# Down projection in batches of six and five chunks, with one ring of small staged parts: attention and a gated FFN on one core

## The chip, the cores and the metric

The kernel runs on one core of a Trainium2 chip. The metric is the device time of one execution in microseconds. Before the change it is 1235.75 us, the median of three runs (1235.59 to 1236.77). The profile is of one execution, and every duration below is from that one.

## What is computed

The reference, cut to its core (B = 1, S = 2048, D = 512, 32 heads of 16, F = 1376, all fp32):

```python
q = (x @ wq).reshape(B, S, H, Dh).transpose(0, 2, 1, 3)
k, v = x @ wk, x @ wv                      # one head of keys and values for all 32
p = softmax(einsum("bhqd,bkd->bhqk", q, k) * Dh ** -0.5)
a = einsum("bhqk,bkd->bhqd", p, v).transpose(0, 2, 1, 3).reshape(B, S, H * Dh) @ wo
b = (gelu(x @ w_gate) * (x @ w_up)) @ w_down
g = sigmoid((x * gate_w).sum(-1, keepdims=True))
return g * a + (1 - g) * b
```

## The kernel before, in words

Each fp32 matrix is held as two halves in a shorter format, high (`...h`) and low (`...l`), and a product is three matmuls: high by high, high by low, low by high. A *split* makes the halves: DVE casts to the high half (L201), and GpSimd (POOL) subtracts it from the source for the low half (L202).

The 2048 rows are four groups of 512. The FFN's 1376 columns are 11 chunks of 128 a group, 44 in all; a chunk has a gate part, an up part (the two *g parts*) and a down part (the *d part*), 256 KB each. The first 80 us make keys, values, queries (which go out to DRAM, `scr`), the first chunk of each group and the first FFN product. Then comes the loop, on which the change works. It interleaves, on TensorE (PE), three streams:

- **S and Z**, scores: two matmuls (L750) fill two PSUM banks with scores of 128 keys by 1024 queries, and ACT takes their exp (L753). S uses the first two pairs of banks in turn, Z the third.
- **V**, values: eight matmuls (L820) add one 128-key step to the attention result. 32 *units* of 16 steps each (four heads by 512 queries) make all 512 steps. When a unit's last V has run, `norm` has DVE copy the result out of its one PSUM bank (L764 or L774) and queues some ten small operations for later.
- **F**, projection steps: a z and a y matmul on the upper and the lower half of PE's rows, side by side (L518).

F steps belong to *jobs*: a **gate job** (24 F) makes one chunk's gate and up products, followed by GELU on ACT and DVE (L543 to L559); a **down job** multiplies a batch of finished chunks by their down weights, for two of the four row tiles of the group, and DVE adds the result to `acc` (L621, L623); a **wo job** (24 F) is the output projection of attention. Batches are of 3, 3, 3 and 2 chunks a group; with two jobs a batch and 3 terms by 2 halves a chunk, a down job has 18 or 12 F.

The second half of a job swaps the two row halves, so that each must wait until both matmul streams of the first half are through. That wait goes over a **relay**: an empty instruction on the SyncE queue (SP) that waits for PE, and that PE waits for in turn (L520 to L529). SP takes its instructions in the order in which they were recorded. It also issues all transfers: weights (L314), pieces of x and wo (L335), the six transfers that load the next unit's queries, called the *Q load* (L363, L364, L369), and the output (L634). The Q load is recorded at the score that is the fifth of a unit's 32.

The order of it all is a list, `PLAN`, one line a job: `H` opens it, `F3` is three F steps, `S`, `Z`, `V2` are as above, `R` closes the job and hands its result to DVE, and `T` starts the GELU's tanh. Visits are unbroken runs of V. After every third F comes a *slot* (L530, L531), in which one queued piece of DVE work is recorded: a split from `todo`, else a piece of wo from `lazy`, else a piece of the norm from `bg`. In the first half of a gate job only the first two of the four slots may take a split.

Weights are staged a chunk at a time, 768 KB in one transfer into one of two buffers (`fetch_w`, L308). A gate job n records the fetch of chunk n + 2 ahead of its first F (L584), and queues the splits of chunk n + 1 two scores later (L587). x and wo come in pieces of 256 KB through two buffers of their own (`fetch_split`, L332).

Of the kernel before, what the change touches and what calls it, by code (L numbers as in the profile page):

```python
# [9 lines left out]
F32 = mybir.dt.float32  # L10
# [4 lines left out]
ALU = mybir.AluOpType  # L15
# [27 lines left out]
PB = 12  # L43
PLAN = [
# [82 lines left out]
def mix_kernel(ctx, tc, xT, wq, wo, wf, out):  # L127
# [51 lines left out]
    st0 = cp.tile([P, 3, D], F32, tag="st", name="st0", bufs=2)  # L179
# [120 lines left out]
    W = {}  # L300
    stage = {0: st0}
# [6 lines left out]
    def fetch_w(n):  # L308
        if n < len(chunks):
            stage[n] = cp.tile([P, 3, D], F32, tag="st", name=f"st{n}", bufs=2)  # L310
            r = chunks[n][1]
            w = wf[(r - 1) % NF].rearrange("p (t d) -> p t d", t=3)
            t0 = 0 if r else 2
            nc.sync.dma_start(stage[n][:, t0:3], w[:, t0:3])  # L314

    def split_w(n):
        if n not in stage:
            return []
        st = stage.pop(n)
        dh = cp.tile([P, D], F32R, tag="dh", name=f"dh{n}", bufs=4)  # L320
        dl = cp.tile([P, D], F32R, tag="dl", name=f"dl{n}", bufs=4)
        parts = [(dh, dl, st[:, 2])]
        gh = gl = None
        if chunks[n][1]:
            gh = cp.tile([P, 2, NC, P], F32R, tag="gh", name=f"gh{n}", bufs=2)
            gl = cp.tile([P, 2, NC, P], F32R, tag="gl", name=f"gl{n}", bufs=2)
            view = lambda t: st[:, t].rearrange("p (c f) -> p c f", c=NC)
            parts = [(gh[:, t], gl[:, t], view(t)) for t in range(2)] + parts
        W[n] = gh, gl, dh, dl
        return [lambda part=part: split(nc.vector, nc.gpsimd, *part) for part in parts]  # L330

    def fetch_split(name, src, dst, queue):  # L332
        def fetch(c):
            t = cp.tile([P, D], F32, tag="xst", name=f"{name}{c}", bufs=2)
            nc.sync.dma_start(t, src[:, c])  # L335
            return t

        parts = {c: fetch(c) for c in range(2)}

        def go(c):  # L340
            hi, lo = dst()
            split(nc.vector, nc.gpsimd, hi[:, c], lo[:, c], parts.pop(c))
            if c + 2 < NC:
                parts[c + 2] = fetch(c + 2)

        queue.extend(lambda c=c: go(c) for c in range(NC))

    def reload_x(tg):
        xs.pop(tg)

        def dst():
            if tg not in xs:
                xs[tg] = x_tiles(tg)
            return xs[tg]

        fetch_split(f"xst{tg}_", xT[tg], dst, todo)
# [19 lines left out]
    def h_tiles(n):  # L376
        return [cp.tile([P, TG], F32R, tag=t, name=f"{t}{n}", bufs=3) for t in ("hh", "hl")]
# [558 lines left out]
```

## Time and profile before

| | us |
|---|---|
| median of three runs (lowest, highest) | 1235.75 (1235.59, 1236.77) |
| the profiled execution's own time | 1235.6 |
| its span, first to last instruction | 1233.8 |
| busy: PE | 1226.5 |
| busy: ACT | 1028.3 |
| busy: DVE | 548.2 |
| busy: POOL | 213.4 |
| span ahead of the loop, loop, end | 80.2, 1137.5, 16.1 |

Busy time is the union of an engine's instructions; a share of 99% says that the engine had always something under way, not that it worked at its peak. A row of the timeline gives start, duration, engine, line, operation, names and shapes, and how many follow each other (xN); brackets hold the idle time ahead of it and what ended it. A row of the waits gives the total, the count and the longest. PEld is PE's weight load, and SPq is SP's own queue.

### The profile page before, as it was taken

To read this page: it belongs to the slowest core of one execution; us is meant where nothing else is said; L and a number is where in the kernel's file an instruction comes from. 1 tells how busy PE (TensorE), PEld (TensorE's weight loads), DVE (VectorE), ACT (ScalarE), POOL (GpSimd) and SP (SyncE) were. 2 spreads that over 40 slices of the span, in tenths; PEclk is the share of its full clock that TensorE was granted. 3 is DMA by queue.
4 is the path that set the end of the run, shared out by engine and by line. 5 is a ranking of instruction groups with operands and counts; after the bars stand their busy time and mean duration, and the time that the engine had idled before them with its cause. 6 is when DMAs were issued, how large, how long until landed. Compare 5 with 4: busy or idle time off the path is not lost.

```text
span 1233.8 us, 23557 instructions
## 1 busy us (share of the span) xinstructions
PE 1226.5 (99%) x9742; PEld 663.7 (54%) x9742; DVE 548.2 (44%) x844; ACT 1028.3 (83%) x1127; POOL 213.4 (17%) x188
## 2 busy tenths in 40 slices
PE   9999999999999999999999999999999999999998
PEld 7875455545454455544545555555555545555555
DVE  7862652533552063543346135343544333344334
ACT  5449899889898888898988888888888888888884
POOL 5411411211220021120222012021123002112100
PEclk9999999999999999999999999999999999999999
DMA  8541202102110110210220012110131011020000
GB/s 332 197 148 57 83 1 66 40 23 99 58 40 15 68 58 15 66 41 23 61 97 27 32 57 66 40 48 33 35 112 45 32 57 60 21 66 27 15 1 35
DMA packets 28317, 73.89 MB, mean 60 GB/s; under 512 B 4208, under 2 KB 4464, under 8 KB 28208
## 3 DMA queue, kind: packets, MB, share of 16 engines
q1 hardware_dynamic: 27664, 71.32, 17.4%
q8 instruction: 77, 1.26, 0.5%
q0 software_dynamic: 256, 0.79, 0.2%
q10 hardware_dynamic: 288, 0.26, 0.1%
q14 instruction: 32, 0.26, 0.1%
HBM read 57.41 MB, written 14.94 MB: 59 GB/s over the span
## 4 chain that ended last, share of the span: by engine, by line
PE 92%; DVE 1%; ACT 1%; issue 0%; ACTq 0%
PE acc L820 38%; PE s L750 23%; PE z L518 15%; PE y L518 15%; PE wos L504 1%; ACT p L753 1%; DVE acc L633 0%; DVE sq L547 0%; PE wof L504 0%; DVE nz L780 0%; DVE sq L546 0%; DVE nt L783 0%; ACT sq L550 0%; DVE gs L543 0%; DVE n L774 0%
## 5 line engine op out<-in xcount | busy, mean ns | idle before, releaser
L753 ACT ACTIVATE p<-s 128x1024 f32<-128x1024 f32 x1024 | 974.9, 1025 | 144.6 <-PE s L750 134.6
L820 PE MATMUL acc<-p,v 128*32 128x512 f32 x4096 | 490.2, 598 | 0.0
L750 PE MATMUL s<-Q,kp 51*128 51x512 f32 x2048 | 376.8, 418 | 1.5 <-DMA Q<-scr 1.2
L750 PEld LDWEIGHTS s<-Q,kp 51*128 51x128 f32 x2048 | 183.1, 184 | 237.4 <-ACT p L753 149.8
L202 POOL TENSOR_TENSOR gl<-st,gh 128x512 fp32r<-128x512 f32 x80 | 112.3, 1423 | 753.1 <-PE s L750 390.8
L820 PEld LDWEIGHTS acc<-p,v 128*32 128x32 f32 x4096 | 110.8, 109 | 244.5 <-issue 236.0
L518 PE MATMUL z<-xh,gh 64*128 64x512 f32 x312 | 123.0, 394 | 0.0
L518 PE MATMUL y<-xh,gh 64*128 64x512 f32 x312 | 123.0, 394 | 0.0
L518 PE MATMUL z<-xl,gh 64*128 64x512 f32 x312 | 122.1, 391 | 0.8 <-POOL xl L202 0.7
L518 PE MATMUL y<-xl,gh 64*128 64x512 f32 x312 | 122.3, 392 | 0.0
L518 PE MATMUL y<-xh,gl 64*128 64x512 f32 x312 | 121.9, 391 | 0.0
L518 PE MATMUL z<-xh,gl 64*128 64x512 f32 x312 | 121.9, 391 | 0.0
L543 DVE COPY gs<-z 128x512 f32<-128x512 f32 x39 | 27.0, 691 | 200.8 <-PE z L518 122.7
L202 POOL TENSOR_TENSOR dl<-st,dh 128x512 fp32r<-128x512 f32 x44 | 57.6, 1309 | 79.9 <-DVE dh L201 50.6
L518 PE MATMUL z<-dh,hh 64*128 64x512 f32 x176 | 69.2, 393 | 0.0
L518 PE MATMUL y<-dh,hh 64*128 64x512 f32 x176 | 69.1, 392 | 0.0
L518 PE MATMUL y<-dl,hh 64*128 64x512 f32 x176 | 68.8, 391 | 0.0
L518 PE MATMUL z<-dh,hl 64*128 64x512 f32 x176 | 68.7, 390 | 0.0
L518 PE MATMUL y<-dh,hl 64*128 64x512 f32 x176 | 68.7, 390 | 0.0
L518 PE MATMUL z<-dl,hh 64*128 64x512 f32 x176 | 68.6, 390 | 0.0
L623 DVE SCALAR_TENSOR_TENSOR acc<-z,gc,acc 128x512 f32<-128x512 f32 x24 | 18.0, 751 | 109.1 <-PE z L518 69.5
L518 PEld LDWEIGHTS z<-xl,gh 64*128 64x128 f32 x312 | 58.1, 186 | 7.4 <-POOL xl L202 1.7
(173 smaller groups left out, 1498.5 us busy)
## 6 DMA issues: line engine op xcount, KB each, us to landing
st<-wf SPq DMA_DIRECT2D x40, 768.0 KB
scr<-q SPq DMA_DIRECT2D x16, 512.0 KB
Q<-scr SPq DMA_DIRECT2D x64, 128.0 KB
Q<-scr SPq DMA_DIRECT2D x64, 64.0 KB
out<-acc SPq DMA_DIRECT2D x16, 256.0 KB
xr<-xT SPq DMA_DIRECT2D x6, 512.0 KB
xst<-xT SPq DMA_DIRECT2D x12, 256.0 KB
st<-wf SPq DMA_DIRECT2D x5, 256.0 KB
```

Source lines behind the costliest of these rows:

```text
L202: eng_l.tensor_sub(lo, src, hi)
L504: nc.tensor.matmul(ps, a, b, start=(first and q == 0), stop=(last and q == len(terms) - 1), skip_group_check=True)
L518: mm = nc.tensor.matmul(ps, a[rs], b[rs], start=(half == 0 and q == 0), stop=(half == 1 and q == len(X) - 1), skip_group_check=True)
L543: nc.vector.tensor_copy(gs, g)
L623: nc.vector.scalar_tensor_tensor(o, ps, w, o, op0=ALU.mult, op1=ALU.add)
L750: nc.tensor.matmul(ps[:, j * TG : (j + 1) * TG], kp[rs, kc * P : (kc + 1) * P], Q[u][rs, pr], start=True, stop=True)
L753: nc.scalar.activation(p, ps, AF.Exp, bias=0.0, scale=SCALE)
L820: nc.tensor.matmul(accp[u][32 * j : 32 * j + 32], vt[:, kc], pb[s, j // 2][:, (j % 2) * TG : (j % 2 + 1) * TG], start=(kc == 0), stop=(kc ...
```

## The change

- Down jobs come in two batches a group, of six chunks (36 F) and five (30 F): 16 down jobs instead of 32, and 61 jobs in all instead of 77. The buffers follow: six pairs of `dh`, `dl` and of `hh`, `hl`, four and three of them in one pool and the rest in another. `acc` has one buffer, not two, and the norm uses `n0` and `n1` in place of `nt`.
- Staging is one ring of four buffers of 256 KB. Its parts are the two g parts of chunk n + 1, the d part of chunk n itself, a piece of wo in four of the jobs, and four pieces of x at a group's end. Three parts are fetched ahead. Splitting a part records the next fetch at once, into the buffer of the part that was split before it.
- Every slot may take a split, and the splits of a job are queued as it opens.
- `PLAN` is written anew, with 1608 F, 1024 S and Z and 512 V as before.

The core of the diff:

```diff
-    "f: H F3 S F3 S F6 S2 F6 S F3 S F3 R S V Z S T S V4 S Z S V2 S",
+    "f: H F3 S F3 S F4 S F2 S F3 S F3 S F3 S F3 R S V S Z T S V4 Z S2 V2 S",
...
+    def parts(n):
+        r = n % NF
+        m = n + 1 if r < NF - 1 else n + 2
+        p = [("g", m, t) for t in range(2)] if m < len(chunks) else []
+        if n > 2:
+            p += [("d", k, 0) for k in ([n] if r > 1 else [n - 1, n])]
+        if 3 <= n < 3 + NC:
+            p.append(("o", 0, n - 3))
+        return p
...
+    def fetch():
+        while supply and len(raw) < STAGE - 1:
+            p = supply.pop(0)
+            t = cp.tile([P, D], F32, tag="st", name="st", bufs=STAGE)
+            nc.sync.dma_start(t, source(*p))
+            raw.append((p, t))
+
+    def split_part(p):
+        q, t = raw.pop(0)
+        assert p == q
+        split(nc.vector, nc.gpsimd, *target(*p), t)
+        done.add(p)
+        fetch()
...
     def slot(split_too):
-        for q in (todo, lazy, bg) if split_too else (bg,):
+        for q in (todo, bg) if split_too else (bg,):
...
                 if q % EVERY == EVERY - 1 and (half == 0 or q + 4 <= len(X)):
-                    slot(half == 1 or q + 6 <= len(X))
+                    slot(True)
...
         def begin():
             flush(todo)
-            if n == 2:
-                fetch_w(3)
-            fetch_w(n + 2)
-            if n == 3:
-                fetch_split("wo", wo, lambda: (woh, wol), lazy)
-            defer(5 if n == 2 else 2, lambda: todo.extend(split_w(n + 1)))
-            if r == NF - 1:
-                defer(3, lambda: todo.extend(split_w(n + 2)))
+            queue_parts(parts(n))
             return weights_terms(n, 0), weights_terms(n, 1)
...
-                acc[tg] = mp.tile([P, 4, D], F32, tag="acc", name=f"acc{tg}", bufs=2)
+                acc[tg] = mp.tile([P, 4, D], F32, tag="acc", name=f"acc{tg}", bufs=1)
...
-            if r % 3 == 2 or r == NF - 1:
+            if r == 5 or r == NF - 1:
```

What this moves shows on SP and on DVE around a gate job that follows the end of a unit. On SP before, in the middle of the loop; `st31` and `st32` are the weights of two chunks, `Q22` the queries of a unit, and the brackets hold what a transfer waits for. The relay itself isn't listed, but its wait for PE is: it stands as PE_49 on the first fetch behind it.

```order
L314 DMA st31_9189<-wf 128x1536 [waits PE_49,DMAHW0_49,Pool_49]
L363 DMA Q22_9200<-scr_71 32x2x512 [waits DMAHW1_49,PE_49]
L364 DMA Q22_9200<-scr_71 16x2x512 [waits DMAHW2_49]
L363 DMA Q22_9200<-scr_71 32x2x512 [waits DMAHW3_49]
L364 DMA Q22_9200<-scr_71 16x2x512 [waits DMAHW4_49]
L369 DMA Q22_9200<-shs_72 3x2x512 [waits DMAHW5_49]
L369 DMA Q22_9200<-shs_72 3x2x512 [waits DMAHW6_49]
L314 DMA st32_9349<-wf 128x1536 [waits PE_49,DMAHW7_49,Pool_49]
```

Between the relay of one job (PE_49 at `st31`) and that of the next (PE_49 at `st32`) stand one fetch, right behind the first relay, and the Q load. On SP after, around a job of the same kind; the `st` rows are single parts.

```order
L349 DMA st_3109<-wf 128x512 [waits PE_49,DMAHW7_49,DMAHW3_49,Pool_49]
L349 DMA st_3124<-wf 128x512 [waits DMAHW4_49,DMAHW0_49,Pool_49]
L367 DMA Q6_3126<-scr_71 32x2x512 [waits DMAHW5_49,PE_49]
L368 DMA Q6_3126<-scr_71 16x2x512 [waits DMAHW6_49]
L367 DMA Q6_3126<-scr_71 32x2x512
L368 DMA Q6_3126<-scr_71 16x2x512
L373 DMA Q6_3126<-shs_72 3x2x512 [waits DMAHW1_49]
L373 DMA Q6_3126<-shs_72 3x2x512 [waits DMAHW2_49]
L349 DMA st_3148<-wf 128x512 [waits DMAHW3_49,Pool_49]
L349 DMA st_3296<-xT 128x512 [waits PE_49,DMAHW4_49,Pool_49]
```

Between the two relays (PE_49 at `st_3109` and at `st_3296`) there are three fetches now, each with a wait for POOL, and the Q load stands between the second and the third. On DVE before, at the job of `st31`: `n020` is the copy of the finished unit's result, `gh30` and `dh30` are high halves of the next chunk.

```order
L764 COPY n020_9180<-acc20_8891 128x512
L765 TENSOR_SCALAR nt20_9181<-n020_9180,mk_80 128x512
L766 TENSOR_SCALAR nz20_9182<-n020_9180,mkb_81 128x512
L201 CAST gh30_9221<-st30_9005 128x512 x2
L201 CAST dh30_9219<-st30_9005 128x512
```

On DVE after, at the job of `st_3124`, with the high halves of chunk 10 and of chunk 9's d part:

```order
L758 COPY n04_3089<-acc4_2815 128x512
L186 CAST gh10_3105<-st_2898 128x512
L186 CAST gh10_3105<-st_2913 128x512
L186 CAST dh9_3144<-st_2930 128x512
L759 TENSOR_SCALAR nz4_3090<-n04_3089,mkb_81 128x512
L760 TENSOR_SCALAR n04_3089<-n04_3089,mk_80 128x512
```

The casts come right behind the copy, ahead of the norm's two products. The copy is still ahead of the casts, and so ahead of POOL's subtractions, on which the fetches above wait.

More of the change, by code (lines that the diff above doesn't have):

```diff
@@ L43 @@
 PB = 12
+STAGE = 4
 PLAN = [
     "t: S2",
[77 rows of a table removed]
[61 rows of a table added]
 ]
@@ L178, in mix_kernel @@
     xr = {tg: p2.tile([P, NC, TG], F32, tag="xr", name=f"xr{tg}", bufs=4) for tg in order[:3]}
-    st0 = cp.tile([P, 3, D], F32, tag="st", name="st0", bufs=2)
+    st0 = p2.tile([P, 3, D], F32, tag="st0", name="st0", bufs=1)
     wf0 = wf[LASTF].rearrange("p (t d) -> p t d", t=3)
@@ L299, in mix_kernel @@
     chunks = [(tg, r) for tg in range(NTG) for r in range(NF)]
-    W = {}
-    stage = {0: st0}
+    G = {}
+    DW = {}
+    todo = []
     now = [-1]
@@ L306, in defer @@
         later.setdefault(now[0] + k, []).append(fn)
[L308 to L356, printed above, removed]
+    def g_tiles(n):
+        G[n] = [cp.tile([P, 2, NC, P], F32R, tag=t, name=f"{t}{n}", bufs=2) for t in ("gh", "gl")]
+    def d_tiles(n):
+        pool, bufs = (cp, 4) if n % 6 < 4 else (mp, 2)
+        DW[n] = [pool.tile([P, D], F32R, tag=t, name=f"{t}{n}", bufs=bufs) for t in ("dh", "dl")]
@@ new lines, in target, with source @@
+    def target(kind, n, c):
+        if kind == "g":
+            if n not in G:
+                g_tiles(n)
+            return [w[:, c].rearrange("p c f -> p (c f)") for w in G[n]]
+        if kind == "d":
+            d_tiles(n)
+            return DW[n]
+        if kind == "x":
+            if c == 0:
+                xs[n] = x_tiles(n)
+            return [x[:, c] for x in xs[n]]
+        return woh[:, c], wol[:, c]
+    def source(kind, n, c):
+        if kind == "x":
+            return xT[n, :, c]
+        if kind == "o":
+            return wo[:, c]
+        t = 2 if kind == "d" else c
+        return wf[(chunks[n][1] - 1) % NF][:, t * D : (t + 1) * D]
@@ new lines, in parts, with x_parts @@
+    def parts(n):
[7 more added lines that the diff above has]
+        return p
+    def x_parts(tg):
+        return [("x", tg, c) for c in range(NC)]
+    supply = [("d", 0, 0), ("g", 1, 0), ("g", 1, 1), ("d", 1, 0), ("g", 2, 0), ("g", 2, 1), ("d", 2, 0)]
@@ new lines, in mix_kernel @@
+    for n, (tg, r) in enumerate(chunks):
+        if r and n > 1:
+            supply += parts(n)
+            if r == NF - 1 and tg + 1 < NTG:
+                supply += x_parts(tg + 1)
+    raw = []
+    done = set()
+    def fetch():
[10 more added lines that the diff above has]
+        fetch()
@@ L358, in mix_kernel, with queue_parts @@
+    def queue_parts(ps):
+        todo.extend(lambda p=p: split_part(p) for p in ps)
     Q = {}
@@ L376, in h_tiles @@
     def h_tiles(n):
-        return [cp.tile([P, TG], F32R, tag=t, name=f"{t}{n}", bufs=3) for t in ("hh", "hl")]
+        pool = mp if n % 2 else cp
+        return [pool.tile([P, TG], F32R, tag=t, name=f"{t}{n}", bufs=3) for t in ("hh", "hl")]
     first = {}
@@ L411, in halves @@
         def halves():
-            hh, hl = h_tiles(NF * tg)
+            hh, hl = h_tiles(0)
             for h in (hh, hl):
@@ L428, in mix_kernel @@
     hold = []
-    fetch_w(1)
+    supply.pop(0)
+    d_tiles(0)
+    fetch()
     for ti, tg in enumerate(order):
@@ L453, in mix_kernel @@
             if ti == 0 and b == 3:
-                split_w(0)[0]()
+                split(nc.vector, nc.gpsimd, *DW[0], st0[:, 2])
+                done.add(("d", 0, 0))
             if ti == 1 and b < 3:
-                if b == 0:
-                    parts = split_w(1)
-                parts[b]()
-                if b == 2:
-                    fetch_w(2)
-            if ti == 2 and b < 2:
-                if b == 0:
-                    parts = split_w(2)
-                parts[b]()
-                if b == 1:
-                    rest = parts[2]
+                split_part((("g", 1, 0), ("g", 1, 1), ("d", 1, 0))[b])
+            if ti == 2 and b < 2:
+                split_part(("g", 2, b))
             if last and b == 2:
@@ L486, in mix_kernel @@
     O = {}
-    todo = []
     bg = []
     chain = []
-    lazy = []
     def slot(split_too):
-        for q in (todo, lazy, bg) if split_too else (bg,):
+        for q in (todo, bg) if split_too else (bg,):
             if q:
@@ L530, in pair_mm @@
                 if q % EVERY == EVERY - 1 and (half == 0 or q + 4 <= len(X)):
-                    slot(half == 1 or q + 6 <= len(X))
+                    slot(True)
                 yield
     def weights_terms(n, t):
-        gh, gl = W[n][:2]
+        assert ("g", n, 1) in done
+        gh, gl = G[n]
         xh, xl = xs[chunks[n][0]]
@@ L594, in end, with flush_down @@
             advance(3)()
-            if r == NF - 1:
-                flush(todo)
-                fetch_w(n + 3)
-                if tg + 1 < NTG:
-                    reload_x(tg + 1)
+            if r == NF - 1 and tg + 1 < NTG:
+                queue_parts(x_parts(tg + 1))
         return begin, end
+    def flush_down(n):
+        while ("d", n, 0) not in done:
+            todo.pop(0)()
     def down_job(batch, i):
@@ L607, in terms @@
             ts = slice(k * P, (k + 1) * P)
-            return [(a[:, ts], b) for n, hh, hl in batch for dh, dl in (W[n][2:],)
+            return [(a[:, ts], b) for n, hh, hl in batch for dh, dl in (DW[n],)
                     for a, b in ((hh, dh), (hh, dl), (hl, dh))]
         def begin():
+            if i == 0:
+                flush_down(batch[-1][0])
             if r == 0 and i == 0:
-                acc[tg] = mp.tile([P, 4, D], F32, tag="acc", name=f"acc{tg}", bufs=2)
+                acc[tg] = mp.tile([P, 4, D], F32, tag="acc", name=f"acc{tg}", bufs=1)
             return terms(i), terms(i + 1)
@@ L637, in begin @@
         def begin():
-            flush(lazy)
+            assert ("o", 0, NB - 1) in done
             flush(bg)
@@ L762, in norm @@
             flush(bg)
-            c0, t, tz = new("n0"), new("nt"), new("nz")
+            c0, tz = new("n0"), new("nz")
             nc.vector.tensor_copy(c0, ac)
-            bg.append(lambda: nc.vector.tensor_scalar(t, c0, mk, None, op0=ALU.mult))
             bg.append(lambda: nc.vector.tensor_scalar(tz, c0, mkb, None, op0=ALU.mult))
-            at[g, b] = c0, t, tz
+            bg.append(lambda: nc.vector.tensor_scalar(c0, c0, mk, None, op0=ALU.mult))
+            at[g, b] = c0, tz
             return
-        r, N, z = at.pop((g, b))
+        N, z = at.pop((g, b))
         last = u == 8 * NTG - 1
+        r = new("n1")
         c1 = ac
         if not last:
-            c1 = new("n1")
+            c1 = r
             nc.vector.tensor_copy(c1, ac)
@@ L868, in gates @@
         nc.vector.tensor_scalar(gt, gt, 0.5, 0.5, op0=ALU.mult, op1=ALU.add)
-    rest()
+    split_part(("d", 2, 0))
     chain.pop(0)()
```

134 rows, old and new, of the table PLAN are left out of this document.

## Prediction, made before the changed kernel ran

> **What bounds the kernel now.** I read the page's busy line and chain first, then the busy time by stretch, then the PE timeline of two ordinary jobs, the waits, and the four engines around one gate job. The page:
>
> ```profile
> PE 1226.5 (99%) x9742; PEld 663.7 (54%) x9742; DVE 548.2 (44%) x844; ACT 1028.3 (83%) x1127; POOL 213.4 (17%) x188
> PE 92%; DVE 1%; ACT 1%; issue 0%; ACTq 0%
> 80.20:1217.70 1137.50, 1136.42 (x9352) 593.61 (x9356) 476.00 (x717) 992.50 (x1065) 179.59 (x134) 1.00 0.15 47
> ```
>
> The third line is the loop: in 1137.50 us PE is busy 1136.42, at a granted clock of 1.00. Busy PE need not be full PE, so I look at the starts. The PE timeline:
>
> ```profile
> 300.44 0.39 PE L518 MATMUL y<-xl,gh 64*128 64x512 f32 x1
> 300.67 0.39 PE L518 MATMUL y<-xh,gl 64*128 64x512 f32 x1
> 300.91 0.40 PE L750 MATMUL s<-Q,kp 51*128 51x512 f32 x2
> 301.14 0.39 PE L518 MATMUL y<-xh,gh 64*128 64x512 f32 x1
> ...
> 302.77 0.40 PE L750 MATMUL s<-Q,kp 51*128 51x512 f32 x2
> 303.10 1.06 PE L820 MATMUL acc<-p,v 128*32 128x512 f32 x8
> 304.10 0.74 PE L750 MATMUL s<-Q,kp 51*128 51x512 f32 x4
> 304.77 1.92 PE L820 MATMUL acc<-p,v 128*32 128x512 f32 x16
> 306.62 0.97 PE L750 MATMUL s<-Q,kp 51*128 51x512 f32 x6
> ```
>
> Columns are start, duration, instruction. From start to start, an F step (a z and a y matmul side by side) takes 0.23 us (300.44 to 300.67) and a score pair S among them 0.23 (300.91 to 301.14). One V step takes 1.00 (303.10 to 304.10), two take 1.85 (304.77 to 306.62): 0.85 each, and 0.15 for each visit, an unbroken run of V. The S before a visit takes 0.33 (302.77 to 303.10), 0.10 more than among F; two S between visits take 0.67 (304.10 to 304.77), 0.21 over two plain ones. So a visit costs 0.15 + 0.21 = 0.36 us beside its steps. The lists of before and after both hold 1608 F, 1024 S and Z and 512 V; before makes 245 visits. 1608 x 0.23 + 1024 x 0.23 + 512 x 0.85 + 245 x 0.36 = 1129 of the 1137.5: PE's own stream is the loop, and anything that stops PE adds its full length. ACT is next:
>
> ```profile
> 307.22 5.64 ACT L753 ACTIVATE p<-s 128x1024 f32<-128x1024 f32 x6
> L753 ACT ACTIVATE p<-s 128x1024 f32<-128x1024 f32 x1024 | 974.9, 1025 | 144.6 <-PE s L750 134.6 <-DVE sq L547 6.4 <-ACT p L753 0.9
> ```
>
> Six exps in 5.64 with a last one of 1.03: 0.92 from start to start, against 3 x 0.23 + 0.23 = 0.92 for "F3 S" on PE. In an F run ACT keeps step to within a hundredth, and outside it waits 134.6 us for PE.
>
> **The change part by part.** *Visits.* The new list has 219 visits, 26 fewer, by keeping V in longer runs: 26 x 0.36 = **-9.4 us**, all on PE's path. No F, S or V goes, so merging batches saves no matmul.
>
> *Reload of x.* Before, x is split during two F12 jobs and PE waits for the last pieces at the first gate job of a group:
>
> ```profile
> 645.18 0.40 PE L518 MATMUL z<-xh,gh 64*128 64x512 f32 x1
> 645.67 0.50 PE L518 MATMUL z<-xl,gh 64*128 64x512 f32 x1
> ...
> 646.24 0.39 PE L518 MATMUL z<-xh,gh 64*128 64x512 f32 x1
> 647.36 0.50 PE L518 MATMUL z<-xl,gh 64*128 64x512 f32 x1 [0.72 <-POOL xl L202]
> ```
>
> 0.49 - 0.23 and 1.12 - 0.23 are lost there, 1.15 us. Two F30 jobs now cover it: **-1.1 us**. Bounds 0 and -1.15; the nearest row is this one.
>
> *Evictions and one acc.* DVE does 32 fewer evictions into acc; it is busy 44% and not in the chain: 0. The output transfers of a group stand two whole jobs ahead of the first write into the same acc: 0. The norm that reuses n0 and n1 has its reads and writes in order on DVE: 0.
>
> *Staging.* This is where I see the price. SP issues 139 weight, x and wo transfers instead of 59, in the same queue as the relay, without which PE can't start a job's second half. 80 issues more at 0.35 us (rows below) are 28 us of SP, free but where a relay stands behind. Two waits:
>
> ```profile
> SPq L314 <- POOL dl L202: 49.2, 16, 6.2
> PEld z L518 <- SPq L526: 1.7, 6, 0.3
> ```
>
> A fetch waits on SP until POOL has done with its buffer, up to 6.2 us, 16 times; yet PE hardly waits for the relay (1.7 us in all). The reason is place: before, the fetch of a gate job is recorded ahead of its first F, so it stands right behind the relay of the job before and has a job's time to wait. After, each split is followed at once by the fetch that takes the buffer of the part split before it, so between H and the relay stand: the fetch behind slot 2 (it waits for POOL's subtraction of the first g part), the fetch behind slot 3 (it waits for the second), and whatever else SP is given there.
>
> [...]
>
> How late is the relay? It depends on when DVE and POOL get to the two g parts. Mostly DVE has run ahead. But where the last visit before H ends a unit, DVE first waits for PE to copy acc (L764). Such a job in before:
>
> ```profile
> 749.85 1.92 PE L820 MATMUL acc<-p,v 128*32 128x512 f32 x16
> 752.04 0.40 PE L518 MATMUL y<-xh,gh 64*128 64x512 f32 x1
> ...
> 755.82 0.40 PE L518 MATMUL y<-xh,gh 64*128 64x512 f32 x1
> ```
>
> ```profile
> 751.84 0.69 DVE L764 COPY n<-acc 128x512 f32<-128x512 f32 x1 [1.00 <-PE acc L820]
> 752.57 0.49 DVE L765 TENSOR_SCALAR nt<-n,mk 128x512 f32<-128x512 f32 x1
> ...
> 753.37 0.75 DVE L201 CAST gh<-st 128x512 fp32r<-128x512 f32 x2
> 753.92 2.79 POOL L202 TENSOR_TENSOR gl<-st,gh 128x512 fp32r<-128x512 f32 x2 [20.43 <-PE s L750]
> ```
>
> ```profile
> 739.76 0.35 SPq L314 DMA_DIRECT2D st<-wf  x1
> 749.49 0.33 SPq L363 DMA_DIRECT2D Q<-scr  x1
> ...
> 751.27 1.49 SPq L369 DMA_DIRECT2D Q<-shs  x2
> 757.98 0.35 SPq L314 DMA_DIRECT2D st<-wf  x1
> ```
>
> The second half starts at 755.82. The six Q transfers take 749.49 to 752.76, 3.27 us of SP, here before the half is due. Put the new order on the same rows. DVE casts the first g part right behind the copy, at 752.57; POOL starts 0.55 later (753.37 to 753.92) and takes 1.40 a part: done at 754.52 and 755.92. SP: the fetch at 754.52 takes 0.35; then the Q load, which the new order puts between the two fetches, 3.27; then the second fetch 0.35: 758.49, and only then the relay. PE is held 758.49 - 755.82 = 2.7 us. With some 0.05 of wait instructions at each of several issues I take **2.9**; ends 2.2 (the subtraction a slot earlier) and 3.3. Queued behind the waiting fetch are the Q load, the next fetch and the relay; who waits is PE, with scores, ACT and V behind it.
>
> How often: of the 39 gate jobs, 18 now follow a visit that ends a unit (12 did before). In 12 of them the Q load falls behind the 6th or 7th F, between the fetches: 12 x 2.9 = 34.8. In one it comes behind the 10th F, after both: 755.92 + 0.35 + 3.27 - 755.82 = 3.7. In five it comes earlier or not at all, and the second fetch alone holds: 755.92 + 0.35 - 755.82 = 0.45, with the same waits 0.6: 3.0. The first gate job has three fetches behind a Q load at the loop's start; no row of before shows that, between 0 and 3.3 I take 2.0, nearer the Q-load case. Sum **+43.5 us**. In the other 20 jobs DVE and POOL are through before H: 0.
>
> *Sum.* Against the profiled execution's 1235.6 (0.15 under the median of the runs): 1235.6 - 9.4 - 1.1 + 43.5 = **1268.6 us**. The 80 us ahead of the loop change in the staging's order alone: 0, within 1.5 either way, as the only wait near is 1.2 us for the first Q:
>
> ```profile
> PE s L750 <- DMA Q<-scr: 1.2, 1, 1.2
> DVE xh L201 <- DMA xst<-xT: 2.2, 1, 2.2
> ```
>
> **The rivals.** *The relay is not held* (0.09): the fetch finds its buffer free, because POOL is earlier than I think. Then only the gains stay: 1235.6 - 10.5 = 1225.1, faster. For it: relays cost 1.7 us in all before, with 12 jobs of this kind. Against: none of those 12 had a fetch of the same job's parts ahead of its relay. It decides where POOL ends its first g part over 3.27 + 2 x 0.35 = 4.0 us before the second half; that would be 751.85, and the copy that precedes it begins at 751.84. The chance stands for what I misread in the order.
>
> *The Q load passes ahead of the fetches* (0.05), so that each of the 18 jobs loses only the 0.6: 1225.1 + 18 x 0.6 + 2 = 1237.9, near no change. For it: in the rows above SP issued Q at 749.49, ahead of H. Against: there the fetch was not before it in the queue.
>
> *Parts land late as well* (0.06): three parts are ahead now, where before two loads of three were. The 2.2 us row above is a split that found its part not landed; say at each of the three group changes and three times more: 1268.6 + 6 x 2.2 = 1282.
>
> The forecast's own case has 0.80, from 1254 (1225.1 + 13 holds of about 2.2, and nothing else) to 1277 (holds of 3.3, and the 1.5 ahead of the loop).
>
> **How the numbers follow.** What can be told from no change here is about 0.2%, 2.5 us. Slower by more: the forecast's case, the third rival and half of the second's chance, 0.80 + 0.06 + 0.02 = 0.88; same 0.03; faster 0.09. The range leaves out the first two rivals (0.14): low 1248, a little under the case's own low end for jobs that I count wrongly, high 1282.
>
> **What would show it.** Right: PE at 96% instead of 99 (some 1216 busy of 1267); a line "z <- SPq" of the relay among PE's waits with 40 us or so and about 19 of 0.4 to 4 us; visits as counted; no gain on ACT, whose wait for PE grows by the same 40 us. The first rival would show relay waits of 2 us in all and PE's loop at 1127 us. Wrong in size: fewer than ten holds over 2 us, or holds near 1. Wrong altogether: a loop longer with PE waiting on ACT, DMA or POOL and not on the relay.

## The result and the profile after

The changed kernel takes 1291.28 us (median of 6 runs, 1290.13 to 1295.39), the kernel before 1236.39 beside it: a ratio of 1.0448 [1.0437, 1.0459]. Slower was forecast, but by 33 us and not by 55: the time lies above the range. The profiled execution after took 1292.77 us with a span of 1291.0, so as much lies outside the loop as before: 1235.6 - 1137.5 = 98.1 and 1292.8 - 1194.7 = 98.1. All that follows is in the loop.

The page of the changed kernel, its busy line, the granted clock over the span and the chain's shares; the last line is the loop in the busy time by stretch (length, then PE, PEld, DVE, ACT and POOL, then the clock).

```profile
PE 1243.3 (96%) x9742; PEld 683.6 (53%) x9742; DVE 571.1 (44%) x812; ACT 1029.8 (80%) x1127; POOL 220.3 (17%) x188
PEclk9999999989999999999999999999999999999999
PE 69%; issue 16%; SPq 3%; POOL 1%; DVE 1%; POOLq 0%
80.20:1274.90 1194.70, 1153.20 (x9352) 613.62 (x9356) 498.51 (x685) 994.00 (x1065) 186.37 (x134) 0.98 0.16 45
```

Two things differ from before. PE stands still for 41.5 us of the loop (1194.70 - 1153.20; it was 1.1). And it is busy for 16.8 us longer (1153.20 against 1136.42) with 26 visits fewer to make, while the clock of the loop is 0.98 and not 1.00. The first was forecast, the second was not. The waits, of PE and of ACT:

```profile
PE z L515 <- SPq L523: 41.0, 18, 3.7
ACT p L747 <- PE s L744: 189.8, 219, 4.5
```

PE waits 18 times for the relay (L523), 41 us in all; ACT's wait for PE is longer by 55 us, so it only follows. One of the 18 places, on SP and then on PE:

```profile
232.18 0.33 SPq L349 DMA_DIRECT2D st<-wf  x1
232.60 0.38 SPq L367 DMA_DIRECT2D Q<-scr  x1
...
234.43 1.49 SPq L373 DMA_DIRECT2D Q<-shs  x2
236.03 0.91 SPq L349 DMA_DIRECT2D st<-wf  x2
```

```profile
233.33 0.47 PE L744 MATMUL s<-Q,kp 51*128 51x512 f32 x2
236.50 0.50 PE L515 MATMUL z<-xh,gh 64*128 64x512 f32 x1 [2.71 <-SPq L523]
236.84 0.39 PE L515 MATMUL z<-xl,gh 64*128 64x512 f32 x1
237.08 0.40 PE L515 MATMUL z<-xh,gl 64*128 64x512 f32 x1
...
237.70 0.62 PE L515 MATMUL z<-xh,gh 64*128 64x512 f32 x1
238.13 0.62 PE L515 MATMUL z<-xl,gh 64*128 64x512 f32 x1
```

This is the forecast's picture: a fetch that waits until POOL has left its buffer (to 232.18), the Q load right behind it (3.3 us of issues), another fetch at 236.03, and only then the relay; the second half starts at 236.50. From start to start 3.17 us pass where a score among F steps takes 0.23: a hold of 2.94. But behind the hold the F steps change: 0.24 from 236.84 to 237.08, then 0.43 from 237.70 to 238.13. Another place, where they don't:

```profile
614.36 0.41 PE L744 MATMUL s<-Q,kp 51*128 51x512 f32 x2
617.52 0.50 PE L515 MATMUL z<-xh,gh 64*128 64x512 f32 x1 [2.75 <-SPq L523]
617.86 0.39 PE L515 MATMUL z<-xl,gh 64*128 64x512 f32 x1
618.10 0.39 PE L515 MATMUL z<-xh,gl 64*128 64x512 f32 x1
```

The two stretches behind these holds, in the busy time by stretch:

```profile
236.60:240.00 3.40, 3.40 (x20) 2.70 (x22) 0.95 (x1) 1.31 (x2) 0.00 (x0) 0.61 0.53 158
617.60:621.00 3.40, 3.40 (x30) 2.78 (x32) 0.95 (x1) 2.17 (x3) 0.00 (x0) 1.00 0.74 186
```

PE counts as busy for all of both stretches, yet does 20 matmuls in one and 30 in the other: the granted clock is 0.61 and 1.00. In the trace's clock record it falls to half eleven times within the loop, for 3.41 us each (once for two such stretches in a row), and all falls lie on one grid of 3.41 us that runs through the whole execution: the eleven begin whole multiples of 3.413 us apart, to within 0.01.

So the 57.2 us by which the loop is longer split like this, from the starts on PE. The 18 holds sum to 44.4. The steps right behind them are longer by 20.0: some 1.65 at each of ten single falls, 2.84 at the double one, 0.10 at each of the seven holds where the clock stays (the expectations below took 20.5). 22 second halves without a hold start 0.13 late, 5 did before: 2.2 (below). The rest, 57.2 - 44.4 - 20.0 - 2.2 = -9.4, is what the visits and the reload of x gave. How long the clock is low differs from one execution to the next: of the six, the one with the highest granted clock (0.987) took 1290.13 us and the one with the lowest (0.980) 1295.39.

### The profile page after: what moved, and what is told of

Its sections match the earlier page's. It is cut to its first block, busy times and chain, and to the rows that moved or that the text cites. A ratio compares the mean times of both kernels' runs of the same rounds, so it can differ in the third digit from the quotient of the medians.

```text
span 1291.0 us, 23739 instructions
## 1 busy us (share of the span) xinstructions
PE 1243.3 (96%) x9742; PEld 683.6 (53%) x9742; DVE 571.1 (44%) x812; ACT 1029.8 (80%) x1127; POOL 220.3 (17%) x188
## 4 chain that ended last, share of the span: by engine, by line
PE 69%; issue 16%; SPq 3%; POOL 1%; DVE 1%; POOLq 0%
PE acc L815 29%; PE s L744 17%; PE z L515 16%; PE y L515 7%; SPq L373 1%; POOL gl L187 1%; SPq L367 1%; SPq L368 1%; SPq L349 1%; PE wos L501 1%; DVE dh L186 0%; DVE acc L627 0%; POOL dl L187 0%; PE wof L501 0%; DVE gh L186 0%
## 5 line engine op out<-in xcount | busy, mean ns | idle before, releaser
L815 PE MATMUL acc<-p,v 128*32 128x512 f32 x4096 | 484.8, 597 | 0.0
L744 PE MATMUL s<-Q,kp 51*128 51x512 f32 x2048 | 390.4, 421 | 1.5 <-DMA Q<-scr 1.4
L515 PE MATMUL z<-xh,gh 64*128 64x512 f32 x312 | 131.4, 421 | 37.3 <-SPq L523 37.3
L515 PE MATMUL y<-xh,gh 64*128 64x512 f32 x312 | 131.3, 421 | 0.0
L515 PE MATMUL y<-xl,gh 64*128 64x512 f32 x312 | 127.5, 409 | 0.0
L515 PE MATMUL z<-xl,gh 64*128 64x512 f32 x312 | 127.4, 408 | 0.0
L515 PE MATMUL z<-xh,gl 64*128 64x512 f32 x312 | 126.8, 406 | 0.0
L515 PE MATMUL y<-xh,gl 64*128 64x512 f32 x312 | 126.8, 406 | 0.0
L515 PEld LDWEIGHTS z<-xh,gh 64*128 64x128 f32 x312 | 61.1, 196 | 56.6 <-SPq L523 47.8
L515 PEld LDWEIGHTS z<-xh,gl 64*128 64x128 f32 x312 | 60.8, 195 | 11.2
```

The lines of the kernel that those rows point to most:

```text
L515: mm = nc.tensor.matmul(ps, a[rs], b[rs], start=(half == 0 and q == 0), stop=(half == 1 and q == len(X) - 1), skip_group_check=True)
L744: nc.tensor.matmul(ps[:, j * TG : (j + 1) * TG], kp[rs, kc * P : (kc + 1) * P], Q[u][rs, pr], start=True, stop=True)
L815: nc.tensor.matmul(accp[u][32 * j : 32 * j + 32], vt[:, kc], pb[s, j // 2][:, (j % 2) * TG : (j % 2 + 1) * TG], start=(kc == 0), stop=(kc ...
```

## The experiments

The theory after the result: holds as forecast; and a stop that leaves PE idle for some 2.0 us of one stretch of the grid halves its clock for the next, at 1.65 us each. The rivals: the slow clock belongs to the new order or to the ring's traffic; POOL, not the queue, is what is late; any stop halves the clock.

### Holds made on purpose in the kernel before

```
     relay = nc.sync.nop(nofuse=True).ins
     ...
+    njob[0] += 1
+    if njob[0] % 2:
+        for i in range(1 + njob[0] // 2 % 9):
+            dump = dr.tile([P, 16], F32, name=f"dump{njob[0]}_{i}")
+            nc.sync.dma_start(dump, ident[:, 0:16])
+        relay = nc.sync.nop(nofuse=True).ins
```

> The kernel before, in its own order of steps, with holds made on purpose: in every second gate or hidden job SP issues 1 to 9 tiny transfers (a 128x16 piece of a constant to a spare place in memory) between its wait for the first half and the relay. Nothing of the computation is left out. At 0.35 to 0.4 us of SP for each, the holds rise in steps of about 0.4 us from 0.2 to 3.4. Theory (what halves the clock is the idle time of PE within one window of a fixed 3.41-us grid, 2.0 us or more; each such window then costs about 1.65 us): no hold under 2.0 is followed by a fall of the clock; holds of 2.0 to 3.4 are followed by one or not, according to where they lie on the grid; each fall lasts 3.41 us and adds 1.5 to 1.8 us to the loop beside the hold. Loop = that of before + sum of holds + 1.65 for each fall. Rival 1 (the clock falls because of the changed kernel's order or traffic): no fall here at any length. Rival 2 (any stop of PE can do it): falls also after holds of 1 us and less.

Measured: 1331.65 us (one run). 36 holds of 0.4 to 4.1 us sum to 72.6; with 23.3 us of longer steps behind them and 0.5 less elsewhere they are the whole 95.4 by which the loop grew. None of the 17 holds under 2.0 us is followed by a fall, 12 of the 19 longer ones are. Two holds of equal length, on PE and in the stretch behind each:

```profile
213.63 0.50 PE L520 MATMUL z<-xh,gh 64*128 64x512 f32 x1 [2.22 <-SPq L536]
213.97 0.39 PE L520 MATMUL z<-xl,gh 64*128 64x512 f32 x1
...
214.91 0.61 PE L520 MATMUL z<-xl,gh 64*128 64x512 f32 x1
215.32 0.63 PE L758 MATMUL s<-Q,kp 51*128 51x512 f32 x2
...
318.30 0.49 PE L520 MATMUL z<-xh,gh 64*128 64x512 f32 x1 [2.23 <-SPq L536]
318.63 0.39 PE L520 MATMUL z<-xl,gh 64*128 64x512 f32 x1
318.86 0.40 PE L758 MATMUL s<-Q,kp 51*128 51x512 f32 x2
```

```profile
213.70:216.40 2.70, 2.70 (x18) 2.19 (x20) 0.00 (x0) 1.36 (x2) 0.00 (x0) 0.73 0.63 183
318.40:321.10 2.70, 2.70 (x24) 2.21 (x26) 0.06 (x1) 1.59 (x2) 2.45 (x2) 1.00 0.67 201
```

Both waited 2.2 us; one halves the clock from 214.91 on, the other doesn't. What parts them is the grid: the first hold lay within one of its stretches, with PE idle there for about 2.1 us, the second across two, with about 1.4 and 1.0. So in the changed kernel: at 236.50 2.6 us of the hold lay in one stretch, at 617.52 1.6 and 1.3 in two. Over this run, the changed kernel and three of the runs below, each of the 26 falls follows a stretch in which PE was idle for about 2 us or more, and no stretch at full clock with clearly more than that went without one. The idle time is worked out from the starts on PE and what a step takes without a stop. By the count used here the smallest with a fall is 1.98 and the largest without one 1.97; the count is good to 0.1 or 0.2 us only, so that the edge is no sharper than "about 2". Two falls, one in each kernel, last for two stretches: there the hold ran on for 0.6 and 0.9 us into a stretch that was already at half clock, where 0.3 us of it or less (three places in this run) brought no second one. The falls come in the order of before too, and not after short stops: the first and the third rival fall.

### Only the Q load behind the relay

```
-            load_q(u + 1)
+            if held[0]:
+                late_q.append(u + 1)
+            else:
+                load_q(u + 1)
```

Here `held` is set in a first half, and the loads in `late_q` are recorded right behind its relay.

> The change as it is, the fetches still ahead of the relay; only the six transfers of a Q load, where they fall in a first half, are recorded behind the relay. Theory (each of the 12 long holds is 0.5 of a second fetch and 2.4 of a Q load queued between the fetches; the clock falls only after holds that leave PE idle for 2 us or more of one 3.41-us window): 13 to 18 holds remain, each 0.5 to 1.7 long, 9 to 13 us in all instead of 44.4; not one window at half clock; 1235 to 1239 us. Rival 1 (any hold on PE, short ones too, halves the clock): still 8 or more half-clock windows, about 1250. Rival 2 (the Q load has no part, the fetches wait for POOL that long by themselves): holds stay at 2.9, and the time above 1280.

Measured: 1240.44 us, a ratio of 1.0034 [1.0021, 1.0047]; 18 holds of 10.3 us in all, 16 of them 0.45 to 0.50, one of 0.98 and the first of 1.66. PE at the place of the first example:

```profile
229.02 0.46 PE L753 MATMUL s<-Q,kp 51*128 51x512 f32 x2
229.73 0.50 PE L518 MATMUL z<-xh,gh 64*128 64x512 f32 x1 [0.25 <-SPq L526]
230.07 0.39 PE L518 MATMUL z<-xl,gh 64*128 64x512 f32 x1
230.30 0.39 PE L518 MATMUL z<-xh,gl 64*128 64x512 f32 x1
```

The hold is 0.48 and the steps behind it are at full speed. The holds are as expected; the time is 1.4 us above the expected 1239. In the profiled execution the clock halved once, behind the first hold, with about 2 us of idle, since PE also idled between the few steps at the loop's start. So the fetches alone hold 0.5, the Q load between them adds 2.4, and with that length the falls go: 51 us for six transfers a few rows further back. The fetches' waits for POOL stand where they stood, so POOL being late is not what makes a hold long: the second rival falls.

### Fetches behind the relay, first try

```
-        fetch()
+        if not held[0] or not raw:
+            fetch()
...
+                    held[0] = False
+                    fetch()
```

> The change as it is, but in the first half of a gate or hidden job each fetch of a weight part is recorded behind the relay instead of ahead of it; the Q load stays where it is. Theory (a fetch that waits on SP ahead of the relay is what holds PE, and the half-clock windows follow from those holds): the 18 holds (44.4 us of the loop in the changed kernel) go, save perhaps one where a Q load comes right ahead of the half; with them go all 11 windows at half clock (20.5 us). What is left is before with 26 visits and one reload less: 1225 to 1228 us, loop 1127 to 1130 us, granted clock 1.00 throughout, relay waits of PE about 2 us in all. Rival 1 (the half-clock windows belong to the new order of steps or to the shared ring of parts, not to the holds): the clock still falls about 11 times and the time is 1243 to 1249. Rival 2 (the holds are POOL being late for the second half itself, the relay only shows it): PE waits for POOL's gl instead of SP, for about as long, and the time stays above 1270. Rival 3 (fetched later, the parts land late): DVE's casts wait for transfers, 1230 to 1240.

Measured: 1243.35 us, 1.0055 [1.0041, 1.0068]: missed. The edit did not do what it was to do. A first half splits three parts, the third left none fetched, and then all three fetches were recorded at once, still ahead of the relay; the Q load came before them. 15 holds are 0.5, one, with the Q load between, is 3.90 and has the one fall of the loop. As a test of the fetches it says what the run above says.

### No fetch ahead of the relay

The same, with the slot rule of before, by which a first half splits two parts:

```
-                    slot(True)
+                    slot(half == 1 or q + 6 <= len(X))
```

> The changed kernel with no fetch at all ahead of a relay: a first half splits two parts and not three (the slot rule of the kernel before), and its fetches are recorded behind the relay. In the earlier run of this kind three fetches stood ahead of 16 relays after all, since the third split left no part fetched; here none does. Theory (only what stands on SP between the halves holds PE): no holds of 0.48 any more, none over 1 but where a Q load alone runs into the half, clock 1.00 throughout, 1230 to 1234 us. Rival (the shared ring with three parts ahead costs by itself, through parts that land late): DVE's casts wait for transfers, 1236 to 1242.

Measured: 1230.94 us, 0.9959 [0.9946, 0.9972]. No hold, no fall. The loop:

```profile
80.28:1212.40 1132.12, 1132.01 (x9356) 600.20 (x9360) 472.20 (x685) 989.99 (x1065) 182.03 (x134) 1.00 0.15 47
```

1137.5 - 1132.1 = 5.4 us faster than before. DVE does wait for parts here, 33.2 us for wo and 27.4 for d in the waits, yet PE is busy 1132.0 of the 1132.1 us: late parts cost nothing here.

### Two parts ahead instead of three

```
-        while supply and len(raw) < STAGE - 1:
+        while supply and len(raw) < 2:
```

> The change as it is, order of recording untouched, but two parts are fetched ahead instead of three, so that with four buffers a fetch takes the buffer of the split before last, which POOL has long left. Theory (what makes the fetch wait is that it takes the buffer that POOL is reading): the fetch behind the first g part no longer waits, the Q load passes SP early, and the fetch behind the second waits for POOL's first subtraction alone, which ends before the half: holds of 0.3 or none, relay waits under 5 us in all, no half-clock windows, 1225 to 1229 us if the parts still land in time. If two parts ahead are too few: the same with DVE waiting for transfers, and PE for DVE's casts, at most 1240. Rival (the number of transfers on SP in front of the relay is what holds it, not a wait of one of them): holds stay near 2.9 and the time near 1290.

Measured: 1234.08 us, 0.9983 [0.9974, 0.9993]. Each fetch takes the buffer of the split before last, so its wait is over a part earlier; the order of recording is untouched. Of the 18 holds one is left, 2.46 us, where the Q load falls late. The rival, that the number of transfers holds the relay, falls. The time is above the expected 1225 to 1229 for three reasons: the 2.46, a loop that begins 1.5 us later than before (PE's first score is at 81.77 instead of 80.23), and 36 times the 0.13 told of below, 4.7.

### Two parts ahead, and the Q load behind the relay

> The version with two parts fetched ahead (1234.1 us), and the Q load recorded behind the relay where it falls in a first half. Theory: that version's one hold (2.46 us, with a Q load between a fetch and the relay) goes, nothing else changes: 1231.4 to 1231.9 us. Rival (a Q load that starts later lands late for its unit's first scores): scores wait for DMA a few times, 1233 to 1240.

Measured: 1230.14 us, 0.9951 [0.9937, 0.9965], no hold in the loop. It is 3.9 us below the version above where 2.5 was expected; in the profiled executions the loop gives 1.0 (1134.4 and 1133.4, this one with one fall at its very start) and the time ahead of it 0.9. Most of the rest is that fall: the profiled execution took 1232.0 at a granted clock of 0.998, the other four 1230.1 to 1230.7 at 1.000.

### Fetches issued by POOL

```
-            nc.sync.dma_start(t, source(*p))
+            nc.gpsimd.dma_start(t, source(*p))
```

> The changed kernel in its recorded order, with the fetches of the shared ring issued by POOL instead of SP. POOL is the engine that frees the buffer, so there the fetch stands behind the subtraction that it waits for. Theory (what holds PE is that the wait for the buffer stands in the queue of the relay): no relay is held by a fetch, the Q load goes early, no window at half clock, relay waits of PE under 5 us in all, 1230 to 1235 us; POOL is busier by 129 x 0.6 = 77 us (0.55 to 0.65 is what POOL's four issues at the start took), which delays its subtractions by one issue each. Rival 1 (POOL's subtractions then come late for PE): waits of PE or PEld for gl, xl or dl instead, above 1240. Rival 2 (a fetch itself, wherever it is issued, slows PE by its traffic): granted clock below 1.00 or F steps above 0.24, above 1240.

Measured: 1236.24 us, 1.0002 [0.9993, 1.0012]. PE no longer waits for the relay and the clock stays, so the theory holds; but the time is above the expected 1235, and 4.5 us are lost in 7 waits for DVE, which were not expected:

```profile
L775 DVE SCALAR_TENSOR_TENSOR nz<-n,mk,nz 128x512 f32<-128x512 f32 x15 | 49.2, 3282 | 0.1
```

In the changed kernel the median of this product is 1.78 us, here 3.96 (0.75 at its shortest in both), with a transfer issued by POOL after each subtraction. DVE comes late to the copy that frees a bank, and the score behind it waits. That POOL's issues stretch DVE's product was seen, not tried by itself.

### Two score steps between the halves

In the runs without holds, 36 second halves start like this (the run with no fetch ahead of the relay; z matmuls left out where y stands):

```profile
139.34 0.39 PE L518 MATMUL z<-xh,gl 64*128 64x512 f32 x1
...
139.58 0.40 PE L749 MATMUL s<-Q,kp 51*128 51x512 f32 x2
139.84 0.50 PE L518 MATMUL z<-xh,gh 64*128 64x512 f32 x1
...
140.18 0.38 PE L518 MATMUL z<-xl,gh 64*128 64x512 f32 x1
```

The score takes 0.26, not 0.23, and the first F step 0.34, not 0.23 or 0.24: 0.13 or 0.14 lost. It is so at all 36 places where one score stands between the halves, and at none of the 25 where two, or a visit, do. Before had 5 of the first kind. SP's relay entry comes 0.43 us after the start of the last F step (the expectation below says its end, which is a slip), and PE starts 0.06 later. The edit moves a score there in these 36 rows of the list, on the version with two parts ahead and the Q load behind the relay:

```
-    "f: H F3 S F3 S F4 S F2 S F3 S F3 S F3 S F3 R S V Z S T S V4 S Z S V2 S",
+    "f: H F3 S F3 S F4 F2 S2 F3 S F3 S F3 S F3 R S V Z S T S V4 S Z S V2 S",
```

> The version with two parts ahead and the Q load behind the relay, with one edit of the list of steps: at the 36 jobs whose halves are parted by a single score step, the score step before it is moved there, so that two stand between the halves (F6 S2 F6 in place of F3 S F3 S F6). Theory (the relay comes 0.43 us after the last F's end, which two score steps cover and one does not: 0.13 us lost at each of the 36, none where two or a visit stand there): 36 x 0.13 = 4.7 us less, 1226.5 to 1227.5 us. Rival 1 (those 0.13 belong to something else at the start of a second half): no gain, 1231 to 1232. Rival 2 (ACT gets its scores 0.7 us later and falls behind, so that PE pays it back at the visits): 1231 or more, with PE waiting for exps.

Measured: 1244.83 us, 1.0073 [1.0059, 1.0087]: slower. The 0.13 is gone at nearly all the places, as the theory had it, but a larger wait came a few F steps later:

```profile
140.52 0.62 PE L753 MATMUL s<-Q,kp 51*128 51x512 f32 x4
...
142.10 0.50 PE L753 MATMUL s<-Q,kp 51*128 51x512 f32 x2 [0.24 <-ACT p L756]
```

Two scores together give ACT two exps, and the next score finds its bank still taken: 0.34 to 0.65 at 35 places, 15.2 us in all. Rival 2, ACT late, is what happened, as the 0.92 against 0.92 of the prediction allows: there is no slack between F3 S on PE and an exp on ACT. The gain would need the scores spread anew, which wasn't tried.

## Why the prediction was right in sign and wrong in size

- **Visits and reload of x**, -10.5: measured -9.4 in the changed kernel (what is left over there), and -9.4 again in the run without holds (-5.4, less 31 x 0.13 = 4.0). Right, a little less per visit: if the reload gave its 1.1, 0.32 and not 0.36.
- **The relay held by a waiting fetch**, +43.5: measured 44.4. Forecast were 12 of 2.9, one of 3.7, five of 0.6 and the first of 2.0; there are 10 of 2.9 to 3.0, 3 of 3.6 to 3.9, 4 of 0.5 and the first of 1.7. So the sum came out by some luck in the counts: two of the 18 gate jobs had no hold, since a visit stands between their halves, and one hold of 3.8 fell in a down job, a kind that was not counted. The shares (0.5 for the fetch, 2.4 for the Q load) are what the run with the Q load moved shows. That a fetch's wait for its buffer held what stood behind it on SP shows in the runs: SP waited 462.0 us for POOL at its fetches (63 times), at the first example until 232.18, with the Q load behind it at 232.60; with the fetches moved to POOL's queue PE no longer waited for the relay, for which it waited 41.0 us in the changed kernel.
- **The failed step** is the sentence "anything that stops PE adds its full length". Here it added more. The prediction priced a hold at its length and the steps behind it at 0.23 us, and nothing in the trace of before showed otherwise: up to the end of its loop the longest stops left PE idle for some 1.5 us of a stretch, at a granted clock of 1.00. What the runs showed in its place is that a stop of 2 us or more can also halve the clock for the stretch behind it, at 1.65 us each: eleven falls, some 20 us. With them the sum would have been 1268.6 + 20 = 1289. Why the trace made no rival of it: the granted clock of 1.00 was read as a property of the kernel, when it hung on PE not stopping for that long: with the holds made on purpose, the same order had 12 falls.
- **Not seen**: second halves parted from the first by a single score, 36 now and 5 before, +2.2 us. The list shows them; the price stood only in the trace's few such places.
- **Evictions, one acc, ahead of the loop**, 0: 98.1 us outside the loop in both. **Parts that land late** (the third rival): not in the changed kernel, and free in the run that had them. **The first rival**'s loop of 1127 is nearly what the run without holds would have had but for the 31 more second halves that start 0.13 late: 1132.1 - 4.0 = 1128.1.

The change does pay once its fetches and the Q load stay out of the relay's way: 1230.1 to 1230.9 us, 0.4 to 0.5% under before.

## What to carry to other kernels

When transfers are moved into a queue that also passes a signal on, look at what each of them waits for: here one waiting fetch held the Q load, the next fetch and the relay behind it, some 2.9 us at a time, and a few rows' order was worth 50 us. Price a stop of PE not at its length alone: here a stop of two or three microseconds could cost half as much again through the clock (1.65 us on 2.9), so that the first aim is to keep stops short. Before moving a step to hide one wait, check that the engine it feeds has slack there: here ACT had none, and 15.2 us were lost where 4.7 were to be gained.

## What the runs showed of the hardware

- PE's granted clock changed on a grid of 3.41 us: each of the 26 falls in five runs came behind a stretch with about 2 us of idle or more, and gave the next stretch 0.5, in which an F step took 0.43 instead of 0.23 us. Cost: about 1.6 us (1.5 to 1.7) for one such stretch beside the stop itself, 2.8 to 2.9 for two in a row. Whether a stop of 2.1 to 3.2 us did it depended on where it lay on the grid: with the holds made on purpose, 2.15 did it at one place and 2.16 and 3.16 did not at others.
- A relay over SP was through 0.43 us after the last F step had begun, and PE started 0.06 later. An F step and one score took 0.46 and did not cover that (0.13 lost at each of 36 places); with a second score, 0.70, they did at nearly all.
- A 128x512 product of two tiles on DVE took 0.75 us alone (2 of its 15 places in the changed kernel), 1.77 to 1.78 beside POOL's subtractions (the other 13), and 3.96 in the median, 3.98 at most, with the fetches on POOL, beside subtractions with a transfer issued by POOL between them.
